# First token tile loaded in two halves by two queues, and the last three products cut into column halves

## The chip, the cores and the metric

The kernel runs on one core of one Trainium2 chip. The metric is the time of one execution on the device, in microseconds (us); a kernel's time is the median of its runs. TensorE (PE) makes the matrix products, with the loading of its weights shown apart (PEld); VectorE (DVE) and ScalarE (ACT) do elementwise work and read the products out of PSUM; GpSimd (POOL) and SyncE (SP) mainly issue transfers. ScalarE can issue transfers too. A name with a q behind it (SPq, ACTq) is the instruction queue of that engine. Transfers of SP show as DMA queue q1, those of ScalarE as q10, those of GpSimd as q0.

## The reference, cut to what matters

One input x of 2048 tokens by 512 channels goes through two branches that a gate mixes:

```python
g = sigmoid((x * gate_w).sum(-1, keepdims=True))
a = s4d_convolution(x)               # long convolution by Fourier transforms
b = einsum("bsf,fd->bsd", einsum("bsd,df->bsf", x, w_gate) * einsum("bsd,df->bsf", x, w_up), w_down)
return g * a + (1 - g) * b           # F = 1792 hidden channels
```

The change touches the second branch, `b`, only: its first loads and its last products.

## The kernel before, in words

All matrix products of branch `b` are made in float32r. To keep precision, each operand is split into a high and a low part (`whi`, `wlo` for the weights of gate and up, `dhi`, `dlo` for those of down, both parts of the tokens in `xs`, `hh` and `hl` for the hidden values), and each product becomes three: high by high, high by low, low by high (`THREE`, line 666). The high part is a copy on ScalarE, the low part a subtraction on VectorE.

Hidden channels go in 14 steps of 128 (`f`), in four groups; tokens go in four chunks of 512 (`ci`). For each step and chunk, `hidden` (line 684) makes 8 `product`s (line 668) of three matrix products: gate into the PSUM tile `pg`, up into `pu`, each over four token tiles `kt` of 128 channels. `down` (line 711) then makes `y` for a row tile `r` of 128 tokens, three products of 512 columns for each step of a group. The convolution's work lies in between; the order of everything is made by a planner (`Work.plan`), from written costs, and issued in that order on every engine.

At the start, `first_loads` (line 577) loads the four token tiles of the first chunk (`xT`, 128 partitions by 512 columns, 256 KB each) and the gate and up weights of step 0 (`w0`) in four pieces, one per `kt`. Piece `kt` holds 128 columns of gate and 128 of up, which in DRAM lie 512 columns apart: two rows of 512 bytes in every partition. SP issues the token tiles and pieces 1 to 3 in turn; ScalarE issues piece 0. In the profile these loads are `y<-in_xT` and `ev<-in_wts`, and `small<-in_rows` is the second transfer that ScalarE issues. While they run, TensorE makes warm-up products of zeros (`k<-acc`). For each `kt`, ScalarE casts the token tile (`xs<-y`), then the weight piece (`whi<-ev`, in `first_split`, line 626); VectorE makes their low parts (`xs<-y,xs` and `wlo<-ev,whi`); TensorE makes six products, the third of which is the first that needs `wlo`.

At the end, the last group's last chunk leaves row tiles in PSUM; `ends` (line 743) adds them to a sum `sums` (`kt` in the profile) that is stored. For the last row tile (`r == 3`) VectorE adds two halves of 256 columns, `acc.t[:, cs]`; the first half is stored by SP, the second by ScalarE (`out<-kt`). Both halves come after the three products of `y` for step 13, which write all 512 columns each.

Every instruction of the kernel is issued through one helper, so line L124 stands for all of them; tiles tell them apart.

Of the kernel before, what the change touches and what calls it, by code (L numbers as in the profile page):

```python
# [18 lines left out]
P = 128  # L19
L, D, N, F = 2048, 512, 128, 1792  # L20
KT = D // P
NF = F // P
NR = L // P
GROUPS = [range(0, 3), range(3, 6), range(6, 10), range(10, 14)]
# [145 lines left out]
class Bus:  # L170
# [25 lines left out]
    def add(self, task, at, us):  # L196
        at = max(at, self.now)
        self.serve(self.queues, self.now, at)
        self.now = at
        self.queues[task.engine == "pool"].append([task, us])  # L200
        self.loads.append((at, sum(x[1] for q in self.queues for x in q)))
        return self.serve([[[*x] for x in q] for q in self.queues], at, 1e9)
# [247 lines left out]
def gated_mix_kernel(  # L450
# [16 lines left out]
    pe, dve, act, sp, pool_q = (InOrder(tc, e) for e in (nc.tensor, nc.vector, nc.scalar, nc.sync, nc.gpsimd))  # L467
# [3 lines left out]
    add = work.add  # L471
# [18 lines left out]
    def new(pool, tag, shape, dtype=F32, bufs=1, loose=False):  # L490
        return work.tile(pools[pool], tag, shape, dtype, bufs, loose)

    def bank():
        return new("ps_k", "k", [P, D], bufs=4, loose=True)
# [71 lines left out]
    def load_two(key, tile_of, src, one=True):  # L566

        t = tile_of([P, 2, D])
        for k in range(2):
            raws[key(k)] = (t, k)  # L570
        if one:
            add("sp", 0.42, lambda: sp.dma_start(t.t, src), w=[t], dma=512, rank=-1)
        return t

    ws, wd, xs = {}, {}, {}

    def first_loads():
        in_y = lambda shape: new("mid", "y", shape, bufs=2)
        in_ev = lambda shape: new("mid", "ev", shape, bufs=2)
        in_in = lambda shape: new("mid", "in", shape, bufs=2)  # L580
        xsrc = lambda kt: xT[P * kt : P * kt + P, :D]
        w0 = raws["w0"] = in_ev([P, 2, D])
        xt = [load_two(lambda k, n=n: ("x", 0, 0, 2 * n + k), in_y, None, False) for n in range(2)]
        wsrc = wts[0][:, : 2 * D].rearrange("p (k d) -> p k d", k=2)
        for kt in range(KT):

            t, k, ks = xt[kt // 2], kt % 2, slice(P * kt, P * kt + P)
            add("sp", 0.42, lambda t=t, k=k, kt=kt: sp.dma_start(t.t[:, k], xsrc(kt)), w=[(t, k)], dma=256, rank=-1)
            e, q = ("sp", sp) if kt else ("act", act)
            add(e, 0.42, lambda q=q, ks=ks: q.dma_start(w0.t[:, :, ks], wsrc[:, :, ks]), w=[(w0, ("k", kt))], dma=128, rank=-1)  # L590
        for f in (1, 2):
            load_two(lambda k, f=f: ("w", f, k), in_ev if f == 1 else in_in, wts[f][:, : 2 * D].rearrange("p (k d) -> p k d", k=2))


        zero = new("glu", "acc", [P, D], bufs=3)
        scratch = bank()
        add("dve", 0.06, lambda: dve.memset(zero.t[:, :P], 0.0), w=[zero], rank=-1)

        def warm():
            w = zero.t[:, :P]  # L600
            for n in (4, 4, 1):
                to = scratch.t[:, : n * P].rearrange("p (n d) -> p n d", d=P)
                rhs = w.unsqueeze(1).broadcast_to([P, n, P])
                pe.matmul(to, w, rhs, start=True, stop=True)

        add("pe", 3.85, warm, r=[zero], w=[scratch], rank=-1, count=12)
# [19 lines left out]
    def first_split(kt):  # L626

        hi, lo, t, k = *ws[0], raws["w0"], ("k", kt)
        cut = lambda x: x.rearrange("p (c d) -> p c d", c=2)[:, :, P * kt : P * kt + P]
        src = lambda: t.t[:, :, P * kt : P * kt + P]  # L630
        add("act", 0.38, lambda: act.copy(cut(hi.t), src()), r=[(t, k)], w=[(hi, k)], rank=0)
        add(
            "dve", 0.42,
            lambda: dve.tensor_tensor(out=cut(lo.t), in0=src(), in1=cut(hi.t).bitcast(F32), op=ALU.subtract),
            r=[(t, k), (hi, k)], w=[(lo, k)], rank=0,
        )
# [28 lines left out]

    THREE = ((1, 0), (0, 1), (0, 0))

    def product(pg, which, w, x, kt, after, first):
        base = which * D + kt * P
        part = ("k", kt) if first else which  # L670

        three = THREE[::-1] if first else THREE

        def fn():
            for n, (a, b) in enumerate(three):
                pe.matmul(
                    pg.t, w[a].t[:, base : base + P], x.t[:, b], start=kt == 0 and n == 0, stop=kt == KT - 1 and n == 2
                )

        add("pe", 0.681, fn, r=[(w[0], part), (w[1], part), x], w=[pg], rank=2, after=after, count=6.16)  # L680

    steps = []

    def hidden(f):

        pg = [new("ps_g", n, [P, D]) for n in ("pg", "pu")]
        x = dict(xs)
        after = T_STEP * len(steps) - 8.0
        steps.append(f)
        pairs = [(which, kt) for which in range(2) for kt in range(KT)]  # L690
        if f == 0:

            pairs.sort(key=lambda p: p[1])
        for which, kt in pairs:
            product(pg[which], which, ws[f], x[kt], kt, after, not steps[1:] and f == 0)
        h = new("glu", "h", [P, D])
        hh, hl = (new("glu", n, [P, D], F32R, SLOTS) for n in ("hh", "hl"))
        add("act", 0.59, lambda: act.copy(h.t, pg[0].t), r=[pg[0]], w=[h], rank=0, urgent=True)
        add(
            "dve", 0.69, lambda: dve.tensor_tensor(out=h.t, in0=pg[1].t, in1=h.t, op=ALU.mult),  # L700
            r=[pg[1], h], w=[h], rank=0, urgent=True,
        )
        add("act", 0.62, lambda: act.copy(hh.t, h.t), r=[h], w=[hh], rank=0, urgent=True)
        add(
            "dve", 0.69,
            lambda: dve.tensor_tensor(out=hl.t, in0=h.t, in1=hh.t.bitcast(F32), op=ALU.subtract),
            r=[h, hh], w=[hl], rank=0, urgent=True,
        )
        return hh, hl

    def down(y, r, h, w, first, last):
        def fn():
            for n, (a, b) in enumerate(THREE):
                pe.matmul(
                    y.t, h[a].t[:, r * P : (r + 1) * P], w[b].t, start=first and n == 0, stop=last and n == 2
                )

        add("pe", 0.681, fn, r=[*h, *w], w=[y], rank=2, count=6.16)

# [58 lines left out]
    def glu():  # L778
        order = [(gi, ci) for gi in range(len(GROUPS)) for ci in (range(4) if gi % 2 == 0 else range(3, -1, -1))]
        tokens(0, 0, 0)  # L780
        weights(GROUPS[0])
        first = new("tab", "kt", [P, 4, D])
        for f in GROUPS[0]:
            raws[("w", f, 2)] = (first, f)
            src = wts[f][:, 2 * D :]
            add("sp", 0.42, lambda f=f, src=src: sp.dma_start(first.t[:, f], src), w=[(first, f)], dma=256, after=9.0 if f == 2 else 0.0)
        down_weights(GROUPS[0])
        old = 0
        for n, (gi, ci) in enumerate(order):
            fs = GROUPS[gi]  # L790
            if ci != old:
                if gi == 0 and ci <= 2:
                    ahead(ci)
                for kt in range(KT):
                    tokens(gi, ci, kt)
            old = ci
            hs = {f: hidden(f) for f in fs}
            ends = n % 4 == 3 and gi + 1 < len(GROUPS)
            if ends:
                weights(GROUPS[gi + 1])  # L800

            for rr in ((0, 1), (2, 3)):
                ys = {r: new("ps_y", "y", [P, D], bufs=2) for r in rr}
                late = fs[-1:] if rr[0] == 0 else []
                for r in rr:
                    for f in fs:
                        if f not in late:
                            down(ys[r], r, hs[f], wd[f], f == fs[0], f == fs[-1])
                    if not late:
                        evacuate(gi, ci, r, ys[r])  # L810
                if late:
                    for r in rr:
                        down(ys[r], r, hs[fs[-1]], wd[fs[-1]], False, True)
                        evacuate(gi, ci, r, ys[r])
            if ends:
                down_weights(GROUPS[gi + 1])
# [675 lines left out]


    first_loads()
    prologue()
    for t in range(NR // 4):
        u_part(t)
    glu()
    v_start()
    amplitudes([0])  # L1500
# [3 lines left out]
    x = x_table(0)  # L1504
    for b in range(NB):
# [5 lines left out]
        if b + 1 < NB:  # L1511
            direct_powers(b + 1)
            leads(b + 1)
            x = x_table(b + 1)
# [59 lines left out]
```

## Time and profile before

| what | value |
|---|---|
| median of 3 runs | 581.37 us (581.23 to 582.0) |
| the profiled execution | 581.93 us |
| its span | 580.1 us |
| TensorE busy | 573.5 us, 99% |
| VectorE busy | 510.9 us, 88% |
| ScalarE busy | 401.6 us, 69% |
| GpSimd busy | 113.5 us, 20% |

The span runs from the first to the last instruction that was recorded on the core; the execution's time lies 1.8 us above it. The times in the rows further down count from the start of the span. A row of the timeline gives start and duration in us, the engine, the operation, output and inputs by name, shapes, how many instructions are merged, and in brackets the idle time before it with what ended it.

### The profile page before, as it was taken

To read this page: it belongs to the slowest core of one execution; us is meant where nothing else is said; L and a number is where in the kernel's file an instruction comes from. 1 tells how busy PE (TensorE), PEld (TensorE's weight loads), DVE (VectorE), ACT (ScalarE), POOL (GpSimd) and SP (SyncE) were. 2 spreads that over 40 slices of the span, in tenths; PEclk is the share of its full clock that TensorE was granted. 3 is DMA by queue.
4 is the path that set the end of the run, shared out by engine and by line. 5 is a ranking of instruction groups with operands and counts; after the bars stand their busy time and mean duration, and the time that the engine had idled before them with its cause. 6 is when DMAs were issued, how large, how long until landed. Compare 5 with 4: busy or idle time off the path is not lost.

```text
span 580.1 us, 14843 instructions
## 1 busy us (share of the span) xinstructions
PE 573.5 (99%) x5998; PEld 433.8 (75%) x5998; DVE 510.9 (88%) x812; ACT 401.6 (69%) x891; POOL 113.5 (20%) x159
## 2 busy tenths in 40 slices
PE   9999999999999999999999999999999999999997
PEld 6777776888886877788677878876868786776775
DVE  6999999999998999999999999997999996347655
ACT  5459888898588589967896775799877544343351
POOL 0003222311111150321132401102333103111011
PEclk9999999999999999999999999999999999999999
DMA  8999959998655797998779757978989439798986
GB/s 284 403 354 358 395 216 354 269 231 232 140 173 128 281 228 173 261 216 273 201 226 250 188 135 238 213 198 206 292 147 292 72 134 289 246 293 222 291 166 128
DMA packets 71687, 136.28 MB, mean 235 GB/s; under 512 B 6852, under 2 KB 35780, under 8 KB 69188
## 3 DMA queue, kind: packets, MB, share of 16 engines
q1 hardware_dynamic: 47668, 87.10, 43.7%
q0 software_dynamic: 23392, 47.98, 39.6%
q8 instruction: 47, 0.77, 0.6%
q10 hardware_dynamic: 560, 0.26, 0.2%
q14 instruction: 20, 0.16, 0.1%
HBM read 80.27 MB, written 55.05 MB: 233 GB/s over the span
## 4 chain that ended last, share of the span: by engine, by line
PE 97%; DMA 1%; ACT 1%; DVE 1%; issue 0%; DVEq 0%; ACTq 0%
PE pg L124 27%; PE y L124 27%; PE pu L124 27%; PE k L124 16%; DMA y<-in_xT 1%; ACT h L124 0%; DVE y L124 0%; ACT acc L124 0%; ACT xs L124 0%; DVE hl L124 0%; DVE dlo L124 0%; DVE kt L124 0%; DVEq L1568 0%; ACT whi L124 0%; DVE h L124 0%
## 5 line engine op out<-in xcount | busy, mean ns | idle before, releaser
L124 PE MATMUL pg<-xs,whi 128*128 128x512 f32 x448 | 138.9, 391 | 0.4 <-ACT whi L124 0.4
L124 PE MATMUL pu<-xs,whi 128*128 128x512 f32 x448 | 138.2, 390 | 0.0
L124 PEld LDWEIGHTS pg<-xs,whi 128*128 128x128 f32 x448 | 84.3, 188 | 17.7 <-ACT whi L124 0.6
L124 PEld LDWEIGHTS pu<-xs,whi 128*128 128x128 f32 x448 | 84.1, 188 | 17.0
L124 PE MATMUL y<-dhi,hl 128*128 128x512 f32 x224 | 90.2, 403 | 0.7 <-DVE hl L124 0.6
L124 PE MATMUL pg<-xs,wlo 128*128 128x512 f32 x224 | 89.9, 401 | 0.8 <-ACT h L124 0.7
L124 PE MATMUL pu<-xs,wlo 128*128 128x512 f32 x224 | 89.3, 399 | 0.0
L124 PE MATMUL y<-dlo,hh 128*128 128x512 f32 x224 | 87.6, 391 | 0.0
L124 PE MATMUL y<-dhi,hh 128*128 128x512 f32 x224 | 87.1, 389 | 0.0
L124 POOL DMA_DIRECT2D out<-acc x44 | 38.5, 930 | 171.6 <-ACT acc L124 171.0
L124 ACT COPY ev<-k 128x512 f32<-128x512 f32 x112 | 59.3, 597 | 15.8 <-PE k L124 13.3
L124 ACT CAST hh<-h 128x512 fp32r<-128x512 f32 x56 | 34.7, 620 | 41.7 <-DVE h L124 41.3
L124 DVE TENSOR_TENSOR h<-pu,h 128x512 f32<-128x512 f32 x56 | 38.6, 689 | 26.3 <-PE pu L124 23.9
L124 ACT ACTIVATE acc<-y,ngate 128x512 f32<-128x512 f32 x62 | 42.0, 689 | 24.3 <-PE y L124 23.2
L124 PEld LDWEIGHTS pg<-xs,wlo 128*128 128x128 f32 x224 | 42.1, 188 | 21.5 <-issue 10.1
L124 PEld LDWEIGHTS y<-dhi,hl 128*128 128x128 f32 x224 | 42.0, 187 | 21.6 <-issue 8.3
L124 ACT COPY h<-pg 128x512 f32<-128x512 f32 x56 | 33.0, 590 | 32.4 <-PE pg L124 28.6
L124 PEld LDWEIGHTS pu<-xs,wlo 128*128 128x128 f32 x224 | 42.0, 188 | 16.7 <-issue 7.0
L124 PEld LDWEIGHTS y<-dhi,hh 128*128 128x128 f32 x224 | 42.1, 188 | 9.0
L124 PEld LDWEIGHTS y<-dlo,hh 128*128 128x128 f32 x224 | 42.1, 188 | 8.1 <-issue 0.3
L124 DVE TENSOR_TENSOR hl<-h,hh 128x512 fp32r<-128x512 f32 x56 | 38.4, 686 | 3.6 <-ACT hh L124 3.1
L124 DVE TENSOR_TENSOR v<-m,v 128x896 f32<-128x896 f32 x32 | 34.0, 1084 | 0.2
(130 smaller groups left out, 959.1 us busy)
## 6 DMA issues: line engine op xcount, KB each, us to landing
xs<-xs_d SPq DMA_DIRECT2D x36, 512.0 KB, 5.8
out<-acc POOLq DMA_DIRECT2D x44, 256.0 KB, 6.4
raw<-in_wts SPq DMA_DIRECT2D x33, 256.0 KB, 4.9
xs_d<-xs SPq DMA_DIRECT2D x16, 512.0 KB, 6.8
su_d<-ev POOLq DMA_DIRECT2D x32, 256.0 KB, 6.1
y_d<-ts SPq DMA_DIRECT2D x28, 256.0 KB, 6.1
in<-su_d POOLq DMA_DIRECT2D x12, 512.0 KB, 8.0
sk_d<-ev SPq DMA_DIRECT2D x6, 1024.0 KB, 3.9
```

The lines of the kernel that those rows point to most:

```text
L124: got = getattr(self.engine, name)(*args, **kw)
```

## The change

There are three edits. First, the first token tile is loaded in two halves of 64 partitions: SP issues partitions 0 to 63 as its first transfer, ScalarE partitions 64 to 127 as its own first one, and piece 0 of the weights after that. Second, on the host the gate and up weights of step 0 are laid out by `kt`, so that each piece is one row of 1 KB in every partition; the casts, the low parts and the products of step 0 address the pieces in that layout. Third, the last `down` of the program (last chunk, `r == 3`, step 13) makes its three products for columns 0 to 255 and then for columns 256 to 511. The planner's list of tasks, their costs and dependencies are the same.

```diff
-        wsrc = wts[0][:, : 2 * D].rearrange("p (k d) -> p k d", k=2)
+        flat = w0.t.rearrange("p k d -> p (k d)")
+
+        def second_half():
+            act.dma_start(xt[0].t[P // 2 :, 0], xsrc(0)[P // 2 :])
+            act.dma_start(flat[:, : 2 * P], wts[0][:, : 2 * P])
+
         for kt in range(KT):
 
-            t, k, ks = xt[kt // 2], kt % 2, slice(P * kt, P * kt + P)
-            add("sp", 0.42, lambda t=t, k=k, kt=kt: sp.dma_start(t.t[:, k], xsrc(kt)), w=[(t, k)], dma=256, rank=-1)
-            e, q = ("sp", sp) if kt else ("act", act)
-            add(e, 0.42, lambda q=q, ks=ks: q.dma_start(w0.t[:, :, ks], wsrc[:, :, ks]), w=[(w0, ("k", kt))], dma=128, rank=-1)
+            t, k, ks = xt[kt // 2], kt % 2, slice(2 * P * kt, 2 * P * kt + 2 * P)
+            cut = slice(0, P if kt else P // 2)
+            add(
+                "sp", 0.42, lambda t=t, k=k, kt=kt, cut=cut: sp.dma_start(t.t[cut, k], xsrc(kt)[cut]), w=[(t, k)],
+                dma=256, rank=-1,
+            )
+            e, fn = ("sp", lambda ks=ks: sp.dma_start(flat[:, ks], wts[0][:, ks])) if kt else ("act", second_half)
+            add(e, 0.42, fn, w=[(w0, ("k", kt))], dma=128, rank=-1)
@@ first_split: the piece's columns
-        cut = lambda x: x.rearrange("p (c d) -> p c d", c=2)[:, :, P * kt : P * kt + P]
-        src = lambda: t.t[:, :, P * kt : P * kt + P]
+        cut = lambda x: x[:, 2 * P * kt : 2 * P * kt + 2 * P]
+        src = lambda: cut(t.t.rearrange("p k d -> p (k d)"))
@@ product: where step 0's weights lie
-    def product(pg, which, w, x, kt, after, first):
-        base = which * D + kt * P
+    def product(pg, f, which, x, kt, after, first):
+        w = ws[f]
+        base = which * D + kt * P if f else 2 * kt * P + which * P
@@ down: the columns in cuts
-    def down(y, r, h, w, first, last):
+    def down(y, r, h, w, first, last, cuts=(slice(0, D),)):
         def fn():
-            for n, (a, b) in enumerate(THREE):
-                pe.matmul(
-                    y.t, h[a].t[:, r * P : (r + 1) * P], w[b].t, start=first and n == 0, stop=last and n == 2
-                )
+            for cs in cuts:
+                for n, (a, b) in enumerate(THREE):
+                    pe.matmul(
+                        y.t[:, cs], h[a].t[:, r * P : (r + 1) * P], w[b].t[:, cs],
+                        start=first and n == 0, stop=last and n == 2 and cs is cuts[-1],
+                    )
@@ glu: which call gets cuts
+        def halves_of(n, r, f):
+            end = n == len(order) - 1 and r == 3 and f == GROUPS[-1][-1]
+            return (slice(0, D // 2), slice(D // 2, D)) if end else (slice(0, D),)
...
-                            down(ys[r], r, hs[f], wd[f], f == fs[0], f == fs[-1])
+                            down(ys[r], r, hs[f], wd[f], f == fs[0], f == fs[-1], halves_of(n, r, f))
@@ host
+    wts[0, :, : 2 * D] = wts[0, :, : 2 * D].reshape(P, 2, KT, P).transpose(0, 2, 1, 3).reshape(P, 2 * D)
```

## Rows read from the trace of the kernel before

**Rows 1.** The page: its head and section 4, the chain by engine.
```profile
span 580.1 us, 14843 instructions
...
PE 97%; DMA 1%; ACT 1%; DVE 1%; issue 0%; DVEq 0%; ACTq 0%
```

**Rows 2.** Chain of waits, 0 to 60 us: start, us, what.
```profile
0.74 3.88 DMA y<-in_xT
...
4.64 0.62 ACT xs L124
...
25.61 0.62 DVE hl L124
```

**Rows 3.** Timeline by engine, 5.0 to 7.0 us: ScalarE, VectorE, TensorE.
```profile
5.17 0.40 ACT L124 CAST whi<-ev 128x256 fp32r<-128x256 f32 x1
5.75 0.62 ACT L124 CAST xs<-y 128x512 fp32r<-128x512 f32 x1 [0.18 <-DMA y<-in_xT]
...
5.90 0.42 DVE L124 TENSOR_TENSOR wlo<-ev,whi 128x256 fp32r<-128x256 f32 x1
...
5.62 1.17 PE L124 MATMUL pg<-xs,whi 128*128 128x512 f32 x2 [0.35 <-ACT whi L124]
...
6.21 0.58 PE L124 MATMUL pg<-xs,whi 128*128 128x512 f32 x1
6.63 0.40 PE L124 MATMUL pg<-xs,wlo 128*128 128x512 f32 x1
```

**Rows 4.** Timeline of the issuing queues, 0 to 2 us; SP's waits to 6 us.
```profile
0.74 0.47 ACTq L124 DMA_DIRECT2D ev<-in_wts  x1
...
1.24 0.49 ACTq L124 DMA_DIRECT2D small<-in_rows  x1
...
SPq L124 <- DMA ev<-in_wts: 1.4, 1, 1.4
```

**Rows 5.** Issues (KB, us to landing); q10, 3.0 to 3.5; a stretch's shares.
```profile
y<-in_xT SPq DMA_DIRECT2D x1, 256.0 KB, 3.9
ev<-in_wts ACTq DMA_DIRECT2D x1, 128.0 KB, 4.3
...
small<-in_rows ACTq DMA_DIRECT2D x1, 2.0 KB, 4.7
...
q10 hardware_dynamic: 104, 0.05, 36.9%
...
4.00:4.50 0.50, 0.50 (x1) 0.11 (x1) 0.00 (x0) 0.00 (x0) 0.00 (x0) 1.00 1.05 337
```

**Rows 6.** Timeline of the tail, 575.9 to 577.5 us.
```profile
575.99 0.39 PE L124 MATMUL y<-dhi,hh 128*128 128x512 f32 x1
576.41 0.88 DVE L124 SCALAR_TENSOR_TENSOR kt<-y,ngate,kt 128x256 f32<-128x256 f32 x2 [1.97 <-PE y L124]
...
577.32 0.36 ACTq L124 DMA_DIRECT2D out<-kt  x1
```

**Rows 7.** DMA queues from 578.0, 578.25 (to 578.5), 578.4, 578.7: packets, MB, share.
```profile
q10 hardware_dynamic: 5, 0.01, 5.8%
...
q10 hardware_dynamic: 80, 0.08, 93.7%
...
q1 hardware_dynamic: 1, 0.00, 0.6%
...
q10 hardware_dynamic: 3, 0.00, 4.0%
```

**Rows 8.** Timeline of ScalarE from 9.5 us and VectorE from 22.9 us.
```profile
9.69 1.14 ACT L124 CAST whi<-ev 128x512 fp32r<-128x512 f32 x2 [0.72 <-DMA ev<-in_wts]
...
23.10 0.69 DVE L124 TENSOR_TENSOR h<-pu,h 128x512 f32<-128x512 f32 x1 [0.26 <-PE pu L124]
```

**Rows 9.** Timeline of TensorE's restart, 570.5 to 571 us.
```profile
570.63 0.19 PEld L124 LDWEIGHTS y<-dhi,hl 128*128 128x128 f32 x1 [0.52 <-ACT acc L124]
...
570.74 0.19 PEld L124 LDWEIGHTS y<-dlo,hh 128*128 128x128 f32 x1
```

More of the change, by code (lines that the diff above doesn't have):

```diff
@@ L694, in hidden @@
         for which, kt in pairs:
-            product(pg[which], which, ws[f], x[kt], kt, after, not steps[1:] and f == 0)
+            product(pg[which], f, which, x[kt], kt, after, not steps[1:] and f == 0)
         h = new("glu", "h", [P, D])
@@ L1540 @@
     by_tile = lambda w: w.reshape(KT, P, NF, P).transpose(2, 1, 0, 3).reshape(NF, P, D)
+    wts = np.concatenate([by_tile(i["B_w_gate"]), by_tile(i["B_w_up"]), i["B_w_down"].reshape(NF, P, D)], axis=2)
+    wts[0, :, : 2 * D] = wts[0, :, : 2 * D].reshape(P, 2, KT, P).transpose(0, 2, 1, 3).reshape(P, 2 * D)
     w1, w1k, w2, w3, w4 = fourier_matrices()
@@ L1544 @@
         "in_xT": host(u[rows.T.reshape(L)].T),
-        "in_wts": host(
-            np.concatenate(
-                [by_tile(i["B_w_gate"]), by_tile(i["B_w_up"]), i["B_w_down"].reshape(NF, P, D)], axis=2
-            )
-        ),
+        "in_wts": host(wts),
         "in_prm": host(
```

## The prediction

> **What bounds the kernel now.** I read the page first: TensorE is busy for almost the whole span and carries 97% of the chain that ended last [rows 1]. A change that leaves the number of products alone can therefore only move two things: when TensorE gets its first operands, and what lies behind its last product. Everything in between follows TensorE's order.
>
> I then read the chain of waits from the start, which gives the head [rows 2]: the first token tile (call it x0) is issued at 0.74 us and landed 3.88 us later, at 4.62; ScalarE casts it at 4.64; the first product starts at 5.62. The timeline of that stretch says what is late at each step [rows 3]. The weight cast follows the token cast on ScalarE at 5.17 without idle time, so the weights were there by then: ScalarE issued them at 0.74 and they landed 4.3 us later, at 5.04 [rows 4, 5]. The third product, the first that needs the low part of the weights, starts at 6.63, after VectorE's low part (5.90 to 6.32). From there TensorE is fed. So two arrivals count: x0 at 4.62, and the first weights (w0) at 5.04, which could come about 0.13 later, 5.17, at no cost at all.
>
> For the tail I read the timeline and the DMA queues [rows 6, 7]. The last full-width product starts at 575.99, lasts 0.39, and VectorE starts on the last row tile at 576.41, in two halves that together take 0.88; ScalarE issues the last store at 577.32, and the span ends at 580.1 [rows 1]. Here TensorE's chain ends, but the DMA engines have work queued: this decides the tail.
>
> **Front: x0 in two halves.** The 256 KB are the same. SP issues partitions 0 to 63, ScalarE 64 to 127, both at 0.74; ScalarE's w0 is no longer its first transfer but its second, at about 1.21 (0.74 plus its issue of 0.47) [rows 4]. What being second on that queue costs has a row: today's second transfer of ScalarE's queue, `small`, has 2 KB, is issued at 1.24 and lands 4.7 us later, at 5.94 [rows 4, 5], just behind the second token tile (x1), whose cast starts at 5.75 when it lands [rows 3]. Two kilobytes can't take that long of themselves: they stood behind x1's 256 KB. The service today thus goes x0, w0, x1, `small`, in turn between the queues. After the change the same turn gives x0's two halves, x1, w0. These are the same 640 KB as x0, w0 and x1 today, and their last byte lands with x1 today: 5.73. So I put w0 at 5.7 instead of 5.04. Its rows of 1 KB instead of two of 512 B save little: 128 packets of 0.047 us (worked out below, from the last store) are 6.0 us over 16 engines, 0.38 us each; the 512-byte ones, from 36.9% of 16 engines for 0.5 us and 104 packets, are 0.028 each [rows 5], 256 of them 0.45 us per engine. That takes 0.07 off: 5.7, rounded.
>
> What x0 itself wins is not in the trace. Upper end of the gain: 128 KB of foreign data in front of it is gone, at the 337 GB/s of 4.0 to 4.5 us [rows 5] 0.39 us. Lower end: ScalarE's half comes behind x1, and x0 lands at 5.73, 1.1 us late. I take no change, 4.62, as the nearest row is x0's own and the DMA engines' share is 1.05 by 4.0 to 4.5 us [rows 5]: they had no free room for two queues to use. The Trainium skill has a rule against such a split ("DMA: Bandwidth & Descriptors", Rules for kernel authors): two transfers to disjoint partition halves share the same engines and serialize, so one transfer of 128 partitions is to be used. By it x0 gains nothing, as assumed; without it the sum would have 4.23 for x0. The share of 1.05 agrees with it.
>
> Now the steps. Token cast 4.64, as before. Weight cast waits for w0: 5.72 to 6.12 (0.40) instead of 5.17. VectorE's low part of the weights: 6.15 to 6.57 instead of 5.90 to 6.32, that is 0.25 later; its low part of x0 is done long before. The first product moves by some 0.55, but the third, which today is held by VectorE, by 0.25: 6.88. Behind the weight cast on ScalarE the x1 cast is queued, 6.02 instead of 5.75, so VectorE's whole row moves by 0.27 as well. TensorE is then fed as today. The shift isn't absorbed later: at 23.10 VectorE waits 0.26 for TensorE [rows 8], so both being 0.25 to 0.27 later just keeps that, and at 25.61 the chain goes over VectorE's `hl` back to TensorE [rows 2]. **Front: +0.25 us.**
>
> **What SP's queue loses.** Of all loads from both queues the ninth waits 1.4 us for w0, the first of them [rows 4], so till 5.04; eight seem to be the limit. One transfer more ahead of it makes the load of the last token tile (x3), today the eighth and not waiting, the one that waits, for a half of x0: issue at 4.64. Today it waits in the engines' backlog anyhow; alone, a tile took 3.9 us [rows 5], which gives 8.5 at worst; VectorE needs it cast at about 9.1. The load that now waits till 5.04 goes to 5.7, and the next step's weights behind it from 9.69 to at most 10.4: ScalarE idles 0.72 for them today [rows 8], VectorE takes them up at 11.1. Cost 0; without that cover up to 0.3. Casts and splits of contiguous 256 columns instead of 2 x 128 stay at 0.40 and 0.42: same elements. Also the ScalarE queue's extra issue (0.47) lies before 4.6, beside its waiting for x0: 0.
>
> **Tail: three products become six of 256 columns.** Half the streaming is 0.11 us; a weight load is needed for each. The nearest row is the restart at 570.63, where two weight loads start 0.11 apart [rows 9]; if loads can follow so closely, the step is about 0.12 and the six take 0.72 instead of 0.68. The other end is the load's full 0.19 plus streaming, 0.3 each: +1.1. I take 0.12. VectorE then starts its first half at 576.08 if the third short product releases it, or at 576.44 if the sixth must be over; the last store is issued at 577.0 or at 577.35. **Neither moves the end.** The last store is 128 rows of 1 KB; 80 packets in 0.25 us at 93.7% of 16 engines make 0.047 us each, and eight per engine 0.37. The last engine leaves SP's queue (the store before) between 578.4 and 578.5 [rows 7]; 578.4 + 0.37 = 578.8, which is when the traffic ends (three packets left in 578.7 to 578.8). That engine goes from one store to the next without a hole, so an earlier issue only queues longer; and as data starts 0.88 after issue (577.32; its first five packets stand at the end of 578.0 to 578.25 [rows 7]), an issue 0.2 later costs nothing either. **Tail: 0**, range -0.15 (holes: the other engines end 0.05 to 0.2 sooner) to +0.9 (1.1 less that slack).
>
> **Sum.** +0.25 + 0 = +0.25. The profiled execution took 581.93, its span 580.1; it becomes 580.35. The median of the runs is 581.37, 0.56 under the profiled execution; the difference goes over to it: 581.6 us. That is 0.04%, far within the 0.2% that a measurement of this kernel can tell from no change.
>
> **Rivals.**
> - *w0 isn't held behind x1* (the queues alternate in small pieces, or ScalarE's second transfer gets in first). For: the two are issued within 0.05 us. Against: `small`. Then 0: 581.4. Chance 0.14.
> - *x0 really lands sooner.* w0 must come by 5.0 too. TensorE could gain 0.39, but VectorE's row hangs on x1, and it is only 0.26 ahead at 23.10: 581.1. Chance 0.10.
> - *ScalarE's half comes behind x1*, x0 at 5.73: every step after moves by 1.1: 582.5. It decides from the point where SP's second load reaches the engines before ScalarE's first. Chance 0.12.
> - *Slower by the clock.* Between the warm-up products and the first real one TensorE idles 0.35 us today [rows 3], after the change 0.9. The column of the granted clock says 1.00, the 2.4 GHz level, from the start [rows 5], but the product at 6.21 lasted 0.58 and the one at 6.63 0.40 [rows 3]: the difference is what half the clock would give (512 columns are 0.43 us at 1.2 GHz, 0.21 at 2.4). If the longer idle stretch leaves TensorE at the low level for the remaining 21 products of the first step, each costs 0.2: up to +4.2, half of it +2.1: 583.7. Chance 0.08.
> - *Tail loses*: loads don't follow so closely, +0.4: 582.0. Chance 0.06.
> - *Tail gains*: the earlier issue reaches the end, -0.33 from 576.41 to 576.08: 581.3 with the front. Chance 0.04. The Trainium skill speaks against its first step ("PSUM — Partial Sum Buffer", PSUM bank collisions raise a hardware error): readers are to be kept off a bank that TensorE writes, whatever the columns. By it VectorE starts at 576.44, not 576.08; no row here shows which.
>
> **How the numbers follow.** The forecast has the remaining 0.46. Faster by over 0.2% (below 580.2) would need more than front and tail hold together (0.39 + 0.15): 0.01. Slower by over 0.2% (above 582.5): the clock 0.08 and a part of x0 coming late: 0.10. Same: 0.89. The range takes in the cases from x0 landing sooner to ScalarE's half behind x1, with 0.2 for the spread of the runs: 580.9 to 582.6.
>
> **What would show it.** Right: x0's cast still near 4.6; the first weight cast waits for its DMA until about 5.7; third product near 6.9; the last store issued at another time but the traffic's end unchanged against TensorE's last product. Wrong: the weight cast again without idle time behind the token cast; x0's cast well before or after 4.6; products of 0.6 us after 7 us; a span that ends sooner by as much as the last store is issued sooner.

## The result: slower by 1.75 us

| | before | after |
|---|---|---|
| median of 22 runs each | 582.24 us | 584.16 us |
| lowest, highest | 581.23, 585.60 | 582.20, 586.69 |
| the profiled execution | 581.93 us | 584.27 us |
| its span | 580.1 us | 582.5 us |

The ratio of the runs is 1.0030, with a 95% interval of 1.0018 to 1.0042. That is 1.75 us more (1.05 to 2.45; the two medians lie 1.92 apart), against a forecast of +0.25. The forecast of 581.6 us started from a median of three runs, 581.37; over 22 runs the kernel before has 582.24, so 0.87 us of the distance from 581.6 to 584.16 is not the change's. Both profiled executions have 1.8 us outside the span, so all of the difference between them lies in the span.

**The start.** The chain of waits of the changed kernel (start, us, what), where [rows 2] stood:

```profile
0.74 4.05 DMA y<-in_xT
...
4.87 1.28 ACT L124
6.15 0.01 issue
6.16 0.62 ACT xs L124
6.78 0.32 ACT whi L124
7.09 0.04 issue
7.14 1.22 PE pg L124 x2
```

Between the landing of the first token tile (x0) and its cast there is a new link of 1.28 us on ScalarE. The groups of instructions say what it is (busy us, mean ns of one, idle time ahead of them and what ended it); first the changed kernel, then the kernel before:

```profile
L124 ACT ACT_TABLE_LOAD x20 | 25.7, 1283 | 5.2 <-DMA y<-in_xT 4.9
```

```profile
L124 ACT ACT_TABLE_LOAD x20 | 25.7, 1283 | 2.1 <-issue 1.8
```

ScalarE loads the tables of its functions 20 times in both kernels, and each takes 1.28 us. In the timeline of the kernel before, the first load stands at 1.75 us, while the transfers were still on their way:

```profile
1.75 1.28 ACT L124 ACT_TABLE_LOAD   x1 [1.75 <-issue]
4.64 0.62 ACT L124 CAST xs<-y 128x512 fp32r<-128x512 f32 x1 [1.60 <-DMA y<-in_xT]
```

It ended at 3.03, and ScalarE then waited for x0 anyway. In the changed kernel the load itself waits for x0. The timelines of ScalarE with its queue (0 to 7.3 us) and of SP's queue (0 to 8 us), where [rows 3, 4] stood:

```profile
0.74 0.57 ACTq L124 DMA_DIRECT2D y<-in_xT  x1
1.35 0.60 ACTq L124 DMA_DIRECT2D ev<-in_wts  x1
1.97 0.45 ACTq L124 DMA_DIRECT2D small<-in_rows  x1
4.87 1.28 ACT L124 ACT_TABLE_LOAD   x1 [4.87 <-DMA y<-in_xT]
6.16 0.62 ACT L124 CAST xs<-y 128x512 fp32r<-128x512 f32 x1
6.68 0.40 ACT L124 CAST whi<-ev 128x256 fp32r<-128x256 f32 x1
```

```profile
0.74 1.47 SPq L124 DMA_DIRECT2D y<-in_xT  x2
...
4.12 0.33 SPq L124 DMA_DIRECT2D y<-in_xT  x1
4.81 1.21 SPq L124 DMA_DIRECT2D ev<-in_wts  x2
```

Why it moved is seen in the program as built, not in a time. These are the first instructions on ScalarE behind its issues, with the semaphores that each waits for, before and after (`DMAHW0` to `DMAHW7` are the eight completion semaphores that the transfers of SP and ScalarE use in turn):

```
before   ACT_TABLE_LOAD
         CAST xs<-y 128x512       [waits DMAHW1: x0]
after    wait                     [waits DMAHW1: SP's half of x0]
         ACT_TABLE_LOAD
         CAST xs<-y 128x512       [waits DMAHW0: ScalarE's half of x0]
```

A cast of two halves needs two transfers. One of its two waits became an instruction of its own ahead of it, and that one stands ahead of the table load too, which belongs to the cast. It is the wait for SP's half, which landed at 4.79; ScalarE's half had landed at 4.11. The Trainium skill has the first half of this ("Perfetto Trace Analysis", Identifying Dependency Chains): for an instruction that waits on several engines, separate waiting instructions may be put in front of it. The listing agrees, with two transfers in place of two engines; that a table load comes behind such a wait is what this case adds.

**From the first product on.** TensorE of the changed kernel, from 5.5 us on:

```profile
7.14 1.22 PE L124 MATMUL pg<-xs,whi 128*128 128x512 f32 x2 [1.87 <-ACT whi L124]
8.15 0.63 PE L124 MATMUL pg<-xs,wlo 128*128 128x512 f32 x1
8.58 1.05 PE L124 MATMUL pu<-xs,whi 128*128 128x512 f32 x2
9.43 0.63 PE L124 MATMUL pu<-xs,wlo 128*128 128x512 f32 x1
...
10.40 0.39 PE L124 MATMUL pg<-xs,wlo 128*128 128x512 f32 x1
...
13.81 0.39 PE L124 MATMUL pu<-xs,wlo 128*128 128x512 f32 x1
14.20 0.50 PE L124 MATMUL pg<-xs,wlo 128*128 128x512 f32 x1
```

In the kernel before, the second step's first product was this one:

```profile
11.81 0.50 PE L124 MATMUL pg<-xs,wlo 128*128 128x512 f32 x1
```

The first product starts at 7.14 instead of 5.62, +1.52: x0's later half landed at 4.79 instead of 4.62 (+0.17), and from there to the cast it takes 1.37 instead of 0.02 (+1.35; the load is 1.28 of it). The 24 products of the first step then last from 7.14 to 14.20, where the second step's first product starts; before, from 5.62 to 11.81. That is 7.06 instead of 6.19, another +0.87, and the rows show where: products last 0.63 until after 9.43, where the kernel before had 0.40 from 6.63 on [rows 3]. The second step is thus 2.39 us late, and at TensorE's restart near the end 2.23 of it is still there.

**The tail.** TensorE's restart and the end, where [rows 9, 6] stood:

```profile
572.86 0.19 PEld L124 LDWEIGHTS y<-dhi,hl 128*128 128x128 f32 x1 [0.52 <-ACT acc L124]
```

```profile
577.76 0.28 PE L124 MATMUL y<-dhi,hl 128*128 128x256 f32 x1
...
577.87 0.28 PE L124 MATMUL y<-dlo,hh 128*128 128x256 f32 x1
...
578.35 0.28 PE L124 MATMUL y<-dhi,hh 128*128 128x256 f32 x1
578.67 0.88 DVE L124 SCALAR_TENSOR_TENSOR kt<-y,ngate,kt 128x256 f32<-128x256 f32 x2 [2.00 <-PE y L124]
579.58 0.36 ACTq L124 DMA_DIRECT2D out<-kt  x1
```

The restart is 2.23 late (572.86 against 570.63). Against that, VectorE's last work comes 0.03 later (578.67 less 2.23 is 576.44, before 576.41) and the end of the span 0.17 later. In this pair the tail took 0 to 0.2 us, not the loss.

### The profile page after: what moved, and what is told of

Read it like the earlier page. It is cut to its first block, busy times and chain, and to the rows that moved or that the text cites. A ratio compares the mean times of both kernels' runs of the same rounds, so it can differ in the third digit from the quotient of the medians.

```text
span 582.5 us, 14851 instructions
## 1 busy us (share of the span) xinstructions
PE 574.2 (99%) x6001; PEld 434.6 (75%) x6001; DVE 511.0 (88%) x812; ACT 400.8 (69%) x891; POOL 113.5 (19%) x159
## 4 chain that ended last, share of the span: by engine, by line
PE 91%; DMA 4%; issue 3%; ACT 1%; DVE 1%; POOL 0%; DVEq 0%; POOLq 0%; ACTq 0%
PE pg L124 26%; PE pu L124 25%; PE y L124 25%; PE k L124 15%; DMA raw<-in_wts 2%; DMA wlo<-in_wts 1%; DMA y<-in_xT 1%; DVE dlo L124 0%; ACT h L124 0%; DVE y L124 0%; ACT L124 0%; ACT v L124 0%; POOL wlo L124 0%; ACT acc L124 0%; ACT dhi L124 0%
## 5 line engine op out<-in xcount | busy, mean ns | idle before, releaser
L124 PE MATMUL y<-dhi,hl 128*128 128x512 f32 (+1 forms) x225 | 90.3, 401 | 0.7 <-DVE hl L124 0.6
L124 PE MATMUL y<-dlo,hh 128*128 128x512 f32 (+1 forms) x225 | 87.6, 389 | 0.0
L124 PE MATMUL y<-dhi,hh 128*128 128x512 f32 (+1 forms) x225 | 87.3, 388 | 0.0
```

The lines of the kernel that those rows point to most:

```text
L124: got = getattr(self.engine, name)(*args, **kw)
```

## The experiments

The theory after the first reading (Theory A in the expectations) was: the second wait pushes the table load behind the token tile (about 1.3 us), and the longer idle stretch of TensorE costs clock (about 0.9). The rivals were the halves and queues themselves (B), the 1-KB rows, and the tail (C). The last three columns come from one trace each, in us; "second step" is its first product, 11.81 before. The differences are the recorded ratios of 5 to 22 runs of a kernel to 17 to 29 runs of the kernel before, turned into us; differences of plain medians lie up to 0.5 from them. The runs come from several chips, so each row is held against runs of the kernel before and not against another row's times.

| kernel | against before, us (95%) | table load | first cast | second step |
|---|---|---|---|---|
| the whole change | +1.75 (1.05 to 2.45) | 4.87 | 6.16 | 14.20 |
| whole change, early table load | +0.65 (0.1 to 1.2) | 2.46 | 4.76 | 13.41 |
| the same, longer warm-up | +0.35 (-0.2 to 0.9) | 2.46 | 4.75 | 13.22 |
| whole change, longer warm-up | +2.3 (1.6 to 3.0) | 4.96 | 6.25 | 13.28 |
| second wait alone | +2.6 (1.9 to 3.3) | 4.57 | 5.87 | 14.50 |
| second wait, early table load | +0.1 (-0.5 to 0.8) | 1.75 | 4.71 | 11.70 |
| halves alone | +2.3 (1.5 to 3.2) | 4.76 | 6.05 | 13.06 |
| halves, early table load | +0.75 (0.1 to 1.4) | 2.49 | 4.95 | 12.00 |
| rows alone | +1.0 (0.2 to 1.7) | 1.66 | 4.82 | 13.38 |
| rows, longer warm-up | +1.1 (0.5 to 1.7) | 1.66 | 4.96 | 11.97 |
| tail alone | +0.4 (-0.3 to 1.2) | 1.77 | 4.52 | 11.71 |
| rows and tail | +0.65 (-0.1 to 1.3) | 1.66 | 5.08 | 13.70 |
| before, longer warm-up | +0.35 (-0.2 to 0.9) | 1.75 | 4.49 | 11.79 |

**The second wait alone.** All transfers as before; VectorE writes one column of the destination first, so that the cast has two things to wait for (the lines that matter):

```diff
+        first = key == ("x", 0, 0, 0)
+        def cast():
+            if first:
+                dve.memset(at(hi, s)[:, :1].bitcast(F32), 0.0)
+            act.copy(at(hi, s), src())
```

> The kernel before, its transfers untouched; VectorE sets one column of the first cast's destination to zero before (about 1 us in), so that this cast has a second thing to wait for. Theory A (a second wait pushes the table load behind the wait for the token tile): the table load starts at 4.6 to 4.8 instead of 1.75, the first cast at 5.9 to 6.1, the first product at 6.9 to 7.1, and the time is the changed kernel's, +1.3 to +2.3 us against before, without any halves, rows or short products. Rival B (halves, queues): no change against before, 0 to +0.1.

Measured: +2.6 us, no less than the whole change. Its timeline of ScalarE (0 to 7.3 us):

```profile
1.23 0.49 ACTq L124 DMA_DIRECT2D small<-in_rows  x1
4.57 1.28 ACT L124 ACT_TABLE_LOAD   x1 [4.57 <-DMA y<-in_xT]
5.87 0.62 ACT L124 CAST xs<-y 128x512 fp32r<-128x512 f32 x1
```

VectorE's column was written at 1.11 us. What was put ahead of the table load was the other wait, that for x0 (`DMAHW1` in the program as built). Neither halves nor a second queue are needed for the loss.

**The same with an early table load.** One more line: a copy of one column of a constant on ScalarE behind its issues, so that the table is loaded there.

```diff
+            act.dma_start(small[:, 0], ...)
+            act.copy(touch, nc.const_aps.tensor_like(0.0, touch))   # touch: one column that nobody reads
```

> The kernel before with the second wait of the first cast (VectorE sets one column of its destination) and with the early table load (a ScalarE copy of one column ahead of the cast). If the place of the table load is all that the second wait costs: the table load at 1.8, the first cast at 4.5 to 4.7, 0.0 to +0.1 us against before. If the wait costs something of itself, or the clock: +1 or more of the +2.6.

Measured: +0.1 us (-0.5 to 0.8). The table load is back at 1.75 and the cast comes as soon as x0 is there:

```profile
1.75 1.28 ACT L124 ACT_TABLE_LOAD   x1 [1.75 <-issue]
3.04 0.19 ACT L124 COPY touch<-const-float32-0.0 128x1 f32<-128x1 f32 x1
4.71 0.62 ACT L124 CAST xs<-y 128x512 fp32r<-128x512 f32 x1 [1.48 <-DMA y<-in_xT]
```

With the pair, the place of the table load is shown to be the whole cost of a second wait, within these intervals. The load itself moved the cast by 1.23 us in the traces (5.87 against 4.64). What the rest of the 2.6 is, the runs don't show: the head of that trace has a stretch of low clock (below), but this kernel was not run with the idle time filled.

**The whole change with the early table load.** The same copy, in the changed kernel.

> The whole change, plus one ScalarE copy of a single column of a constant behind its three DMA issues, which makes it load its table of functions there. Theory A (the second wait of the first cast holds the table load back, and the longer idle stretch of TensorE keeps its clock at the low level): the load of 1.28 us starts at 2.4 instead of 4.87, the first token cast at 4.83 instead of 6.16, the first product at 5.8 instead of 7.14, full-rate products from about 7 us on; the second step's first product, 2.39 us late in the changed kernel, is at most 0.3 late, and the profiled time is 582.2 (582.27 is 584.27 less 2.0). Theory A without the clock (the low level has another cause): only 1.3 comes back, 583.0. Rival B (the two halves themselves, their queues and the issues that became slower, cost the time): nothing comes back, 584.2.

Measured: +0.65 instead of +1.75; of the change's loss 1.1 us came back, from two separate comparisons with about 0.6 us to either side each. The pair with the longer warm-up (below), made on one chip, gives it more clearly: +2.3 with the late table load, +0.35 with the early one (and two warm-up products fewer). The cast came as forecast (4.76, for 4.83), the first product 0.26 after its forecast (6.06, as the first weights landed only at 5.58), and in the trace the second step was still 1.6 late, with another cause; this execution took 584.49 where 582.2 was expected. ScalarE, from 6.8 us on, and the second step:

```profile
8.75 0.41 ACT L124 CAST whi<-ev 128x256 fp32r<-128x256 f32 x1 [0.27 <-DMA ev<-in_wts]
11.73 1.14 ACT L124 CAST whi<-ev 128x512 fp32r<-128x512 f32 x2 [2.57 <-DMA ev<-in_wts]
12.77 0.58 ACT L124 COPY h<-pg 128x512 f32<-128x512 f32 x1
...
13.41 0.50 PE L124 MATMUL pg<-xs,wlo 128*128 128x512 f32 x1 [1.61 <-ACT h L124]
```

The second step's weights (9.69 in [rows 8]) came at 11.7, and behind their cast ScalarE has the first step's result, which frees TensorE's bank. A second trace of the same kernel:

> The first experiment once more, for its trace. In two kernels with the early table load and the halves the cast of the second tile's weights began at 11.73 and 11.55, in three with a late table load and halves at 10.04 to 10.34, in five without halves at 9.60 to 9.69. If the halves always put it past 11 us when the table is early: again 11 or later, and the second step 1.4 or more late. If that was chance: about 10.2, and the second step at most 0.6 late.

Again 11.72, and the second step at 13.39. The two profiled executions took 584.49 and 584.45 us, but the other eleven runs 581.77 to 583.43. So this late landing, though it came twice, seems not to be what the median pays; how often it comes without a profile stays open.

**One part at a time.** The three parts of the change were made alone, each with the kernel before for all else: the halves with the weights' old rows, the rows (with the products and casts that read them) with x0 whole and issued by SP, and the tail by `cuts` and `halves_of` as in the change. In short, for the first pieces:

```diff
+ halves:  sp.dma_start(t.t[: P // 2, 0], xsrc(0)[: P // 2])
+          act.dma_start(xt[0].t[P // 2 :, 0], xsrc(0)[P // 2 :])
+          act.dma_start(w0.t[:, :, ks], wsrc[:, :, ks])
+ rows:    q.dma_start(flat[:, ks], wts[0][:, ks])
```

> The kernel before with the first token tile in two halves alone: the first weights stay in 512-byte rows, the last three products stay at full width. Theory A: the table load starts at about 4.85 behind the wait for one half, the first token cast at 6.15, the first product at 7.1, and the time is the changed kernel's less what its tail costs (0 to 0.15): +2.1 against before. Rival (the 1-KB rows and the other order of the weight's columns matter): 0 to +0.3. If the 512-byte rows make the first weights land later than 5.0, up to 0.1 shows in no place, since the table load covers them.

> The kernel before with the first weights in 1-KB rows alone (one row of 256 contiguous columns for each partition, casts and products read accordingly). Theory A: the table load stays at 1.75, the first weights land at 5.04 less up to 0.07, the first cast stays at 4.64: 0.0 against before. Rival (the longer rows crowd out the first token tile on the DMA engines): the first cast after 4.8 and +0.2 to +0.4.

> The kernel before with the last three products cut into two halves of the columns alone. Theory A: the six follow each other at 0.12 us, VectorE starts 0.03 later against TensorE's schedule, the last DMA lands 0 to 0.17 later: 0 to +0.17 us against before. Rival C (the tail carries the change's loss): +1 to +2. Rival of the purpose (the earlier half is used early): -0.3.

The halves alone cost +2.3, the table load late as forecast. The tail alone gave +0.4, with zero inside the interval, and its trace had the six products at steps of 0.12, as the whole change. The rows alone cost +1.0, where 0.0 was expected, and their first cast was late (4.82), as the rival said, though its +0.2 to +0.4 was too small. Two more kernels took this apart:

> The kernel before with the first token tile in halves and the early table load, without the 1-KB rows and the short products. If the halves hold the 0.65 us that were left (x0 0.1 to 0.3 later, the second tile's weights later): +0.4 to +0.7. If the rows hold it: 0 to +0.3. If the halves are the gain that they look like (x0 sooner): below 0.

> The kernel before with the 1-KB rows and the short products, without the halves: the two parts that measured +1.0 (+0.2 to +1.7) and +0.4 (-0.4 to +1.2) alone. If they add up: +1.4. If the 0.65 us left in the first experiment are theirs: +0.6. If both are noise: 0 to +0.2.

Halves with the early table load: +0.75, so by the difference of two wide intervals 1.55 of the 2.3 was the table. Rows and tail together: +0.65. Each of these two would by itself explain the 0.65 that the early table load had left; they don't add up to it, and the intervals are too wide to share it out.

What they have in common is a later x0. The last of the 16 completion marks of its transfer (of the later half, where there are two) stands in the traces at 4.46 to 4.63 in six executions with x0 whole and weights in 512-byte rows (mean 4.53), at 4.80, 4.94 and 5.06 in the three with x0 whole and 1-KB rows, and at 4.51 to 5.05 in the eight with halves (mean 4.77). Neither edit made x0 come sooner: it was 0.4 later with the rows and 0.24 later with the halves (six of those eight have the rows too; the two without have 4.69 and 4.87). In seven of the eight it was SP's half that came last; ScalarE's landed at 3.90 to 4.51.

**The clock.** TensorE's clock has two levels, 1.2 and 2.4 GHz (0.50 and 1.00 in the rows). Where TensorE idles longer before its first products, the low level can last longer. In the kernel with the second wait the record of the granted clock shows it; busy time by stretch (us, busy and count of each engine, then the granted clock, DMA share, GB/s):

```profile
5.20:6.84 1.64, 0.00 (x0) 0.00 (x0) 0.33 (x1) 1.63 (x4) 0.00 (x0) 1.00 1.08 358
6.84:8.26 1.42, 1.42 (x5) 0.94 (x6) 1.42 (x4) 1.42 (x4) 0.00 (x0) 1.00 1.10 387
8.26:11.68 3.42, 3.42 (x10) 2.67 (x9) 3.25 (x15) 2.15 (x5) 0.00 (x0) 0.50 1.01 368
11.68:14.50 2.82, 2.82 (x13) 1.99 (x11) 1.55 (x5) 0.64 (x2) 0.00 (x0) 1.00 0.97 318
```

```profile
8.95 1.06 PE L124 MATMUL pg<-xs,whi 128*128 128x512 f32 x2
9.80 0.63 PE L124 MATMUL pg<-xs,wlo 128*128 128x512 f32 x1
```

TensorE stood idle from 5.12 to 6.84; at 8.26 the clock fell to 0.50, the 1.2 GHz level, though TensorE was busy by then, and came back at 11.68. The timeline ties the 0.63 us of a product to that level. Products of 0.63 in the changed kernel thus ran at 1.2 GHz, though the profile's column says 1.00 there. The trace's record of the granted clock says why: its first entry starts at 10.01 us in the changed kernel, at 6.60 in the kernel before and at 9.74 with the rows alone, and where there is no entry the column prints 1.00. In each of these traces products go from about 0.6 to 0.40 where the record starts. To see whether this is fixed or drawn anew, both kernels were traced a second time:

> The whole change once more, for its trace. Fixed by the change: table load at 4.8 to 5.0, first cast at 6.1 to 6.3, first product at 7.0 to 7.3. If the clock of the head is drawn anew in each execution: the second step's first product anywhere from 13.0 (1.2 late) to 14.5 (2.7 late). If not: 14.2 again.

> The kernel before once more, for its trace. Table load at 1.7 to 1.8, first cast at 4.45 to 4.65, first product at 5.4 to 5.65, cast of the second tile's weights at 9.6 to 9.7. If the stretch from 354 to 447 us differs by chance between executions, the last product comes 0 to 1.5 us later than in the first trace though the head is the same.

The changed kernel had the same late table load (5.12) and cast (6.42), but the clock fell for 9.00 to 12.41, and the second step came at 15.04 instead of 14.20. The kernel before had its second step at 11.96 (11.81) and its last product 0.37 later than in the first trace, so the middle differs little in that pair. It can differ more: the kernel before with the longer warm-up had the second step at 11.79 and its last product 1.28 later. The ends of single traces are therefore not compared here below such a size, but their heads are. In the four kernels with a late table load the second step stands at 13.06, 13.28, 14.20 and 14.50: the first, with 1.76 us of idle time, had no low level at all after it. The length of the idle stretch doesn't decide it either: with the rows alone TensorE idled 0.54 us and stayed at the low level until 9.74. An idle stretch allows the loss; it doesn't force it. Four kernels were then given more warm-up products, to fill the idle time:

```diff
-            for n in (4, 4, 1):
+            for n in (4, 4, 4, 1):       # the whole change
+            for n in (4, 4, 3):          # the whole change with the early table load
+            pe.matmul(scratch.t[:, : 3 * P // 4], w, w[:, : 3 * P // 4], ...)   # the kernel before, 96 columns more
```

> The whole change, with four more warm-up products, so that TensorE is busy until about 7.0 instead of 5.27. The table load stays late (4.87) and the first product at 7.1. Theory A with the clock (the late first product costs about 1.5 and the longer stay at the low level the rest, as TensorE stood idle for 1.87 us): the clock is at its full level no later than 8 us in, and +1.3 to +1.5 against before instead of +1.75 to +2.3. Theory A without the clock (the time of the rise is chance and the same for both): no gain, +1.75 against before. If the warm-up runs over the first product, it shows as a product later than 7.2.

> The whole change with the early table load of the first experiment and two more warm-up products (0.86 us), so that TensorE is busy until about 6.1. Theory A with the clock: of the 0.65 us that were left with the early table load alone, what the clock took is regained: 0 to +0.3 against before. Without it: +0.65. A cost that neither touches: the load of the second tile's weights, one load further behind the limit of eight, lands later than 9.7 and ScalarE casts it ahead of the first step's result; where it lands at 10.3 or sooner it costs nothing, at 11.7 it costs 1.6.

> The kernel before with one more warm-up product of 96 columns (about 0.32 us), so that TensorE is busy until about 5.6, when its first operands come. If short idle stretches of TensorE in the head keep the clock low in part of the executions: -0.3 to -1.0 against before, and a narrower spread of the runs. If the rise of the clock has nothing to do with the 0.35 us of idle time: 0.0.

> The kernel before with the first weights in 1-KB rows and one more warm-up product (0.43 us), so that TensorE is busy until about 5.7 and the first product comes at 5.8. The rows alone took +1.0 us (+0.2 to +1.7), of which 0.18 was a later first cast; in their profile the clock was at the low level until 9.74, after an idle stretch of 0.54. If that clock is the rest: +0.2 against before, and a full clock by 8 us. If the rows cost something else: +1.0 again.

(The last one, the rows alone, has one more block of 128 columns.) In two of the four the products didn't fill the stretch: in their traces the clock rose at 4.80 and 4.87, the rest of the warm-up ran at the high level, and TensorE still idled 1.27 us in the whole change (1.87 without) and 0.58 with the rows (0.54 without). In the other two no idle time was left there. In the trace of the first, full-rate products came from 7.2 us on and the second step at 13.28, 0.9 sooner than in the change; with the rows they came from 5.94 on and the second step at 11.97, 1.4 sooner than without. No median moved clear of its interval: +2.3 against +1.75, +0.35 against +0.65, +0.35 against 0, +1.1 against +1.0. So the clock's part is seen in single executions, up to 1.5 us of the head (7.66 us from the first product to the second step in the kernel with the second wait, 6.19 before), but on the median it is smaller than these intervals of about 0.6 us to either side, or the filler costs what it brings. For the rows the expectation had named the two outcomes: a full clock and +1.0 again mean that they cost something else. The clock isn't shown to be part of the 1.75.

No version run here is faster than the kernel before by more than its interval.

## Why the prediction was wrong, step by step

- **"Token cast 4.64, as before": wrong, and this is the step that failed.** The prediction weighed the landing of two halves and took the cast to follow at once. It didn't ask what else the instruction carries that waits: the second wait took the table load from a place where it cost nothing (1.75 to 3.03, ScalarE idle until 4.64) into the chain: the cast came at 6.16. The prediction names the work that hides other work for several edits; for this load it didn't, as no step touched it in the diff. With the load back in its early place, the second wait cost 0.1, and the whole change 0.65. What makes up these 0.65 stays open.
- **x0's landing unchanged (4.62): nearly right.** 4.79 in the pair, 0.24 later on the mean of eight traces. No gain of 0.39 appeared in any, and no half came behind x1, as a rival had it. The Trainium skill's rule against two disjoint partition halves ("DMA: Bandwidth & Descriptors", Rules for kernel authors) was right for this: the split gains nothing.
- **w0 behind x1 at 5.7: wrong.** Its completion marks end at 4.97, ahead of x1 at 5.68, although it was issued as its queue's second transfer. The row of `small`, on which the step rested, doesn't carry over to it. The front's +0.25 was thus the wrong term, and the rival "w0 isn't held behind x1" happened, without its 581.4. In the whole change with the early table load w0 came at 5.58 and 5.61, in the other six traces with halves at 4.85 to 5.22. In one of the eight it did land behind x1 (5.61 and 5.15), so the order is not fixed.
- **The 1-KB rows at no cost (0.07 off w0): the sign wrong.** The rows alone measured +1.0 (0.2 to 1.7), with x0 0.4 later. The prediction counted the time of packets of w0 alone and not what it takes from the transfer beside it. Not all of the +1.0 is thereby explained.
- **SP's queue: right while the table load was late, too small in the whole change without it.** Eight is the number of completion semaphores in the program as built, as the prediction had read it from the waits. x3's load waited for a half of x0 (ScalarE's, 4.11) and was issued at 4.12, the second step's weights were cast at 10.04 instead of 9.69 with slack left: nothing lost. "Without that cover up to 0.3" was too small: 1.4 to 1.6 in the three traces of the whole change with the early table load. With the halves alone and the early load the weights were cast at 10.23, and the second step was 0.19 late.
- **Tail 0: nothing speaks against it.** Steps of 0.11 to 0.12 as taken from [rows 9], and VectorE's first half was not released by the third short product but only after the sixth: 578.67, which is the 576.44 of the prediction moved by 2.23. The cause is in the program as built: of the six products only the last one raises the semaphore for which VectorE's first half waits. The prediction cited the Trainium skill ("PSUM — Partial Sum Buffer", PSUM bank collisions raise a hardware error) for readers being kept off the bank that TensorE writes. The time agrees, but no run here puts that rule to the test, as the program never let the first half start sooner. Measured by itself: +0.4 (-0.3 to 1.2), so a cost of some tenths isn't excluded.
- **The rival "slower by the clock" had the nearest time (583.7) with a chance of 0.08.** Its mechanism is in the trace: products of 0.63 after 7 us, +0.87 in the head. It was also right to doubt the 1.00 of the clock's column. But the idle stretch was 1.87 and not 0.9, for a reason that it didn't have, and the median doesn't show its share; that its time came nearest is luck.
- **Range and chances.** The upper end, 582.6, came from x0 a whole transfer late (581.37 + 1.1, with 0.2 for the spread, is rather 582.7); no case had a late ScalarE for another reason than a landing. A slower outcome by over 0.2% had 0.10.

## What to carry to other kernels

Splitting a load gives its first reader a second wait. In the programs built here the cast carried one wait, and the other stood ahead of everything that belongs to the cast, a table load of 1.28 us among it. Before such an edit, look for what stands directly ahead of the reader at no cost today, and pin it to an early place with one tiny instruction (here a copy of one column, which brought +2.6 us back to +0.1). A transfer that isn't on the critical path can still take from the one beside it: with longer rows for the weights the tokens landed 0.4 later.

## What the runs showed that was not expected

- A single wait more on one cast, with no change to any transfer: +2.6 us (1.9 to 3.3).
- Weights in rows of 1 KB instead of two of 512 bytes let the 256-KB tile beside them land at 4.80 to 5.06 instead of 4.46 to 4.63. The traces bear out that the weights' queue took more of the early traffic: of the packets from 0.7 to 3.5 us, ScalarE's queue (q10) had 0.10 MB in the three traces with 1-KB rows, and 0.05 to 0.06 MB in the six with 512-byte rows. Why longer rows get more wasn't tested.
- SP's first two issues took longer in the kernels in which ScalarE issued the other half of the tile beside them: 1.21 to 1.47 us in eight traces, 0.86 to 0.87 in the nine others.
- The granted clock fell to 0.50 from 8.26 to 11.68 while TensorE was busy, after an idle stretch from 5.12 to 6.84. In the second trace of the changed kernel it fell from 9.00 to 12.41, after 2.13 us of idle time that ended at 7.39.
